# Rows of the input loads cut into two to six pieces, with a DRAM layout to match

## The chip, the cores and the metric

The kernel runs on one core of a Trainium2 chip. The metric is the device time of one execution, in microseconds (us). One profiled execution gives the trace; its clock starts at the first instruction.

## The reference

Three parts follow each other (float32 throughout): chunked attention with a few memory keys, a gated product without an activation, and a second feed-forward part with a SoLU and a layer norm.

```python
# attention: q, k, v (4, 8, 768, 64), mem_k, mem_v (4, 8, 8, 64); for each chunk of 32 queries:
scores = 0.125 * q_c @ concat(mem_k, k[chunk - 16 : chunk + 32 + 8]).T
a = exp(scores - max) ; a = a / (sum(a) + 1e-9) ; out_c = a @ concat(mem_v, v_ctx)
# x = out as (3072, 512)
x = ((x @ w_a) * (x @ w_b)) @ w_out            # d_ff 1536
h = x @ w_in                                    # 512 -> 1024
solu = h * softmax(h)
y = ((solu - mean) / sqrt(var + 1e-6) * g_ln) @ w_out2
```

## The kernel before

**Number format.** A float32 product is made of three passes with operands that are split into a high part and a rest (`w_hi` on ScalarE copies the high part, `w_lo` on VectorE subtracts it). The weights arrive as raw float64 words (512 of them are 4 KB) and are turned into float32 on the chip by integer steps: `abs` and `low` on ScalarE, `shl`, `sign` (or `join`) and `add` on VectorE, through a buffer `Z` with two halves that the weights use in turn, even and odd.

**Stages.** The first feed-forward part has 12 blocks f of 128 hidden columns. For each f there is one weight tile `raw` of 128 partitions by 1536 words (12 KB a partition, 1.5 MB): w_a, w_b and w_out side by side. The function `front` works on the first 512 tokens and converts all 12 weights on the way: products `pa`, `pb` with block f, the copy of the first product to `G` (step `G`), the gate (step `gate`), and the product `x` with w_out. Weights 0 and 1 come in three parts each (512 words a partition, 0.5 MB), weights 2 to 11 whole. The order of all this on TensorE, VectorE and ScalarE is written out by hand in the table `ORDER` (lines 45 to 66).

**Attention groups.** A group is 128 queries of all 8 heads: a query-key tile of 128 x 1280 float32 (5 KB a partition) and a value tile of 128 x 1024 (4 KB). Its steps are S (scores on TensorE), M (maximum and subtraction on VectorE), X (exponential on ScalarE), N (sums on VectorE, multiplication on VectorE or GpSimd), T (transposes on TensorE), A, V, C, L. Groups 0 to 3 run at the start, 4 to 7 inside `front`. After it pairs of groups are loaded by `pair_load`.

**Loads.** All loads and most stores are issued by SyncE in the order of the program; the data go through one queue over 16 DMA engines. Eight semaphores are used in turn, so a DMA is not issued before the eighth one ahead of it has landed. The first loads are, in order: qk0, qk1, weight 0 part 0, qk2, v0, weight 0 part 1, qk3, v1, weight 0 part 2, v2, weight 1 part 0, v3, weight 1 parts 1 and 2, weights 2, 3, 4, two stores of converted weights, weight 5, a store, weights 6 to 11, qk4, v4, qk5, then stores of converted weights (`w1_store`, lines 538 and 540), and the step `whole7` (line 517), which stores a third of `Z` to `woz`. The step `abs9` (line 421) writes that half of `Z` again, so it waits for that store.

Of the kernel before, what the change touches and what calls it, by code (L numbers as in the profile page):

```python
# [18 lines left out]
P = 128  # L19
B, H, S, D = 4, 8, 768, 64  # L20
# [3 lines left out]
NCH = 4  # L24
GQ = NCH * CQ
WQ = 2 * CQ
KW = 96
GK = GQ // WQ * KW
NG = S // GQ
NP = H // 2  # L30
DM = H * D
DFF1 = 1536
DFF2 = 1024
NF1 = DFF1 // P
# [4 lines left out]
WC = 512  # L39
# [33 lines left out]
NS = 3  # L73
# [7 lines left out]
def fused_kernel(  # L81
# [9 lines left out]
    nc = tc.nc  # L91
# [22 lines left out]
    def ld_tile(n, name):  # L114
        return ld_p.tile([P, n], F32, tag="ld", name=name, padded_shape=[P, NP * (GQ + GK)])
# [31 lines left out]
    def flat(t):  # L147
        return t.rearrange("p a c -> p (a c)")

    quads = {}  # L150
    rest = {}
    xt = {}
# [2 lines left out]
    def slot_tile(i, shape, dtype, name):  # L155

        return wp.tile(shape, dtype, tag=f"w{i}", name=name)
# [8 lines left out]
    def att_load(qi, slot=None):  # L166


        n = NP * (GQ + GK) + NCH * NP * D
        q, k = NP * GQ, NP * (GQ + GK)  # L170
        if slot is None:

            t = ld_tile(k, "qk")
            tv = ld_tile(n - k, "v")
        else:
            t = slot_tile(slot, [P, n], F32, "qkv")
            tv = t[:, k:n]
        nc.sync.dma_start(t[:, 0:k], qkv[qi, :, 0:k])
        quads[qi] = dict(
            q=t[:, 0:q].rearrange("d (p t) -> d p t", p=NP),  # L180
            k=t[:, q:k].rearrange("d (p t) -> d p t", p=NP),
            v=tv.rearrange("k (c p d) -> k c p d", c=NCH, p=NP),
        )

        def values():
            nc.sync.dma_start(tv, qkv[qi, :, k:n])

        if slot is None:
            values()
        return values  # L190

    def att_P(qi):
        full = ps_at.tile([P, 2, 512], F32, tag="at", name="s")
        s = full[:, :, 0:NP * CK].rearrange("q r (p k) -> q r p k", p=NP)
        if qi % NG == 0:
            nc.vector.memset(s[0:CQ, :, :, 0:16], NEG)
        if qi % NG == NG - 1:

            zero = ident[GQ - CQ:GQ, 0:8 * H].rearrange("q (r p k) -> q r p k", r=2, p=NP)
            nc.scalar.activation(  # L200
                out=s[GQ - CQ:GQ, :, :, 56:64], in_=zero, func=AF.Copy, scale=0.0, bias=NEG
            )
        quads[qi]["s"] = s

    def att_S(qi):


        st = quads[qi]
        g = qi % NG
        s = st["s"]  # L210
        for p in range(NP):
            for c in range(NCH):
                lo = 16 if (g == 0 and c == 0) else 0
                hi = 56 if (g == NG - 1 and c == NCH - 1) else CK
                k0 = (c // 2) * KW + (c % 2) * CQ
                for r in range(2):
                    rows = slice(64 * r, 64 * r + 64)
                    nc.tensor.matmul(  # L218
                        s[CQ * c:CQ * c + CQ, r, p, lo:hi],
                        st["q"][rows, p, CQ * c:CQ * c + CQ],  # L220
                        st["k"][rows, p, k0 + lo:k0 + hi],
                        start=True,
                        stop=True,
                    )
# [87 lines left out]
    def pair_load(d, i, values):  # L312

        qi = 2 * d + i
        n = NP * (GQ + GK) + NCH * NP * D
        q, k = NP * GQ, NP * (GQ + GK)
        if values:
            t = ld_tile(n - k, "v")
            nc.sync.dma_start(t, qkv[qi, :, k:n])
            quads[qi]["v"] = t.rearrange("k (c p d) -> k c p d", c=NCH, p=NP)  # L320
        else:
            t = ld_tile(k, "qk")
            nc.sync.dma_start(t, qkv[qi, :, 0:k])
            quads[qi] = dict(
                q=t[:, 0:q].rearrange("d (p t) -> d p t", p=NP),
                k=t[:, q:k].rearrange("d (p t) -> d p t", p=NP),
            )
# [149 lines left out]
    raws = {}  # L477
# [4 lines left out]
    def cols(part):  # L482
        return slice(0, NS * WC) if part is None else slice(part * WC, (part + 1) * WC)

    def w1_load(f, part=None):
        if f not in raws:
            raws[f] = slot_tile(f + 5 if f < PARTED else f, [P, NS * WC], I64, "raw")
        nc.sync.dma_start(raws[f][:, cols(part)], w1d[f, :, cols(part)])

    def w1_z(f, part=None):  # L490
        if f not in zs:
# [446 lines left out]
    def ab(bi, f, which, lo=0, hi=TB, ps=None, ks=range(NP)):  # L938
        xh, xl = xt[bi]
        w = wa1[f, which]  # L940
        if ps is None:
            ps = ps_ab.tile([P, TB], F32, tag=f"ps{which}", name="pab")
        sl = slice(lo, hi)
        for k in ks:
            mm3(ps[:, sl], w[:, 0, k], w[:, 1, k], xh[:, k, sl], xl[:, k, sl], k == 0, k == NP - 1)
        return ps
# [18 lines left out]
    def x2_step(bi, f, gh, gl, ms=range(NP)):  # L965
        if f == 0 and ms[0] == 0:
            acc[bi] = [ps_acc.tile([P, TB], F32, tag="acc", name="acc") for _ in range(NP)]
        w = wo1[f]
        for m in ms:
            sl = slice(m * P, (m + 1) * P)  # L970
            mm3(acc[bi][m], w[:, 0, sl], w[:, 1, sl], gh, gl, f == 0, f == NF1 - 1)
# [320 lines left out]
    values = {}  # L1292
# [21 lines left out]
    def front():  # L1314
        half = TB // 2
        psum = {}
        gates = {}
        started = {}
        q_end, k_end = NP * GQ, NP * (GQ + GK)

        def product(f, which, part):
            cols_, ks = started.get((f, which), (0, 0))
            if part == "l":
                started[f, which] = half, 0
                psum[f, which] = ab(0, f, which, 0, half)
                return
            to = NP // 2 if part == "h" else NP
            started[f, which] = cols_, to
            psum[f, which] = ab(0, f, which, cols_, ps=psum.get((f, which)), ks=range(ks, to))

        def add_x2(f, part):
            x2_step(0, f, *gates[f], ms=range(NP // 2) if part == "h" else range(NP // 2, NP))

        def group_S(q):
            if "s" not in quads[q]:
                att_P(q)
            att_S(q)

        def group_N(q):
            att_N(q, nc.vector if q < n0 else None)  # L1340

        def group_T(q):
            att_T(q, *((ps_ab, f"ps{q % 2}") if q < n0 else ()))

        def group_V(q):
            att_V(q, *((ps_acc, "acc") if q < n0 else ()))

        def load_qk(q):
            t = ld_tile(k_end, "qk")
            nc.sync.dma_start(t, qkv[q, :, 0:k_end])  # L1350
            quads[q] = dict(
                q=t[:, 0:q_end].rearrange("d (p t) -> d p t", p=NP),
                k=t[:, q_end:k_end].rearrange("d (p t) -> d p t", p=NP),
            )

        def load_v(q):
            n = NCH * NP * D
            t = ld_tile(n, "v")
            nc.sync.dma_start(t, qkv[q, :, k_end:k_end + n])
            quads[q]["v"] = t.rearrange("k (c p d) -> k c p d", c=NCH, p=NP)  # L1360

        def first(f):
            nc.scalar.copy(G0, psum[f, 0])  # L1363

        def second(f):
            gate_by(psum[f, 1])

        def gate_h(f):
            gates[f] = gate_hi(f)

        def gate_l(f):
            gate_lo(*gates[f])

        steps = dict(
            P=att_P, S=group_S, M=att_M, X=att_X, N=group_N, T=group_T, A=att_A, V=group_V, C=att_C, L=att_L,
            abs=w1_abs, neg=w1_neg, low=w1_low, shl=w1_shift, sign=w1_sign, join=w1_join,
            add=w1_add, hi=w1_hi, lo=w1_lo,
            G=first, gate=second, gh=gate_h, gl=gate_l,
            pa=lambda f, part=None: product(f, 0, part), pb=lambda f, part=None: product(f, 1, part),
            x=lambda f, part=None: add_x2(f, part),  # L1380
            loadw=w1_load, loadqk=load_qk, loadv=load_v,
            store=w1_store, whole=w1_whole,
            loadp=lambda i: pair_load(2 * NDIR, *((0, False), (1, False), (0, True))[i]),
        )
        def perform(item):
            name, *which = item.split(".")
            kind = name.rstrip("0123456789")
            steps[kind](int(name[len(kind):]), *(int(i) if i.isdigit() else i for i in which))

        for item in ORDER.split():  # L1390
            perform(item)
# [80 lines left out]
    for sb in range(NSB):  # L1472
        n = BASE[sb]
# [39 lines left out]
    for sb in range(NSB):  # L1513
# [24 lines left out]
        for p in range(HF):  # L1538
            a, b = order.index((2, p)), order.index((1, p))
# [82 lines left out]
    for sb in range(NSB):  # L1622
# [6 lines left out]
        for f in range(NF1):  # L1629
# [16 lines left out]
            v = bank_of("v", g)  # L1646
# [273 lines left out]
```

## Time and profile before

| | us |
|---|---|
| median of 3 runs (lowest to highest) | 874.55 (873.86 to 874.86) |
| the profiled execution's own time | 873.66 |
| its span, first to last instruction | 871.8 |
| TensorE busy | 855.4 (98%) |
| VectorE busy | 700.2 (80%) |
| ScalarE busy | 401.7 (46%) |
| GpSimd busy | 66.8 (8%) |

The shares are means over stages with different limits. The page has a row on the chain of work that ended last; the table by stretches shows what each engine does in each ten microseconds; the list of waits and the timeline show who waited for whom. Times of rows count from the span's start; 1.9 us of the execution lie outside the span.

### The profile page before, as it was taken

To read this page: it belongs to the slowest core of one execution; us is meant where nothing else is said; L and a number is where in the kernel's file an instruction comes from. 1 tells how busy PE (TensorE), PEld (TensorE's weight loads), DVE (VectorE), ACT (ScalarE), POOL (GpSimd) and SP (SyncE) were. 2 spreads that over 40 slices of the span, in tenths; PEclk is the share of its full clock that TensorE was granted. 3 is DMA by queue.
4 is the path that set the end of the run, shared out by engine and by line. 5 is a ranking of instruction groups with operands and counts; after the bars stand their busy time and mean duration, and the time that the engine had idled before them with its cause. 6 is when DMAs were issued, how large, how long until landed. Compare 5 with 4: busy or idle time off the path is not lost.

```text
span 871.8 us, 16681 instructions
## 1 busy us (share of the span) xinstructions
PE 855.4 (98%) x6696; PEld 707.3 (81%) x6696; DVE 700.2 (80%) x1136; ACT 401.7 (46%) x601; POOL 66.8 (8%) x79
## 2 busy tenths in 40 slices
PE   5999999999999999999999999999999999999998
PEld 4887878888888888888888888888888888888887
DVE  6999965978876685777957778999589999998892
ACT  5986432434343332334836544266354444444432
POOL 0001000000000000000000000000322223322110
PEclk9999999999999999999999999999999999999999
DMA  9997554967799679863889998468903555553343
GB/s 367 412 424 302 193 165 176 303 206 244 259 364 400 264 265 398 326 220 125 291 284 377 331 332 316 164 238 280 315 25 105 162 166 177 157 187 123 121 150 129
DMA packets 96542, 214.49 MB, mean 246 GB/s; under 512 B 7760, under 2 KB 58704, under 8 KB 91344
## 3 DMA queue, kind: packets, MB, share of 16 engines
q1 hardware_dynamic: 96432, 213.42, 68.9%
q8 instruction: 53, 0.87, 0.4%
q14 instruction: 25, 0.20, 0.1%
q0 software_dynamic: 32, 0.00, 0.0%
HBM read 147.85 MB, written 65.54 MB: 245 GB/s over the span
## 4 chain that ended last, share of the span: by engine, by line
PE 93%; DVE 4%; DMA 1%; ACT 1%; issue 1%; POOL 0%; ACTq 0%; DVEq 0%; POOLq 0%
PE acc L833 26%; PE pab L1275 15%; PE acc L1053 13%; PE pab L804 7%; PE acc L804 5%; PE pab L934 5%; PE pab L935 4%; PE pab L936 4%; PE acc L934 2%; PE acc L935 2%; PE acc L936 2%; PE px L399 2%; PE s L218 2%; PE px L287 1%; PE pab L833 1%; DMA w<-wos 1%
## 5 line engine op out<-in xcount | busy, mean ns | idle before, releaser
L833 PE MATMUL acc<-w 128*128 128x512 f32 x978 | 227.4, 390 | 0.0
L833 PEld LDWEIGHTS acc<-w 128*128 128x128 f32 x978 | 182.7, 188 | 38.1
L1275 PE MATMUL pab<-w 128*128 128x512 f32 (+1 forms) x600 | 134.3, 381 | 0.0
L1275 PEld LDWEIGHTS pab<-w 128*128 128x128 f32 x600 | 109.4, 188 | 21.9 <-DVE w L1252 0.3
L1001 POOL TENSOR_TENSOR w2ld<-w2ld 128x256 f32<-128x256 f32 x44 | 38.8, 902 | 528.5 <-ACT r L824 480.3
L934 PE MATMUL pab<-x,w 128*128 128x512 f32 (+1 forms) x200 | 78.7, 394 | 0.0
L935 PE MATMUL pab<-x,w 128*128 128x512 f32 (+1 forms) x200 | 76.9, 384 | 0.0
L936 PE MATMUL pab<-x,w 128*128 128x512 f32 (+1 forms) x200 | 76.8, 384 | 0.0
L804 PE MATMUL pab<-w 128*128 128x512 f32 x288 | 70.2, 390 | 0.2 <-DMA w<-wos 0.2
L846 DVE TENSOR_TENSOR part<-acc,part 128x512 f32<-128x512 f32 x56 | 38.6, 690 | 37.2 <-PE acc L833 28.4
L804 PEld LDWEIGHTS pab<-w 128*128 128x128 f32 x288 | 53.8, 188 | 11.7 <-ACT w L775 0.5
L1053 PE MATMUL acc<-w,hx 128*128 128x512 f32 x252 | 60.6, 390 | 0.1
L1053 PE MATMUL acc<-w 128*128 128x512 f32 x252 | 60.3, 390 | 0.0
L1053 PEld LDWEIGHTS acc<-w,hx 128*128 128x128 f32 x252 | 47.1, 188 | 10.2 <-DVE mx L1069 0.5
L1053 PEld LDWEIGHTS acc<-w 128*128 128x128 f32 x252 | 47.1, 188 | 9.7
L804 PE MATMUL acc<-w 128*128 128x512 f32 x216 | 51.7, 389 | 0.0
L804 PEld LDWEIGHTS acc<-w 128*128 128x128 f32 x216 | 40.5, 188 | 8.4
L934 PEld LDWEIGHTS pab<-x,w 128*128 128x128 f32 x200 | 38.1, 191 | 7.7 <-ACT G L1363 0.2
L936 PEld LDWEIGHTS pab<-x,w 128*128 128x128 f32 x200 | 38.1, 191 | 7.3
L935 PEld LDWEIGHTS pab<-x,w 128*128 128x128 f32 x200 | 38.2, 191 | 6.7
L779 DVE TENSOR_TENSOR w<-r,w 128x512 fp32r<-128x512 f32 x56 | 37.7, 688 | 1.9 <-ACT w L775 1.9
L934 PE MATMUL acc<-gh,w 128*128 128x512 f32 x96 | 38.2, 398 | 0.0
(234 smaller groups left out, 1392.4 us busy)
## 6 DMA issues: line engine op xcount, KB each, us to landing
w<-ws SPq DMA_DIRECT2D x24, 1024.0 KB, 7.3
w<-ws SPq DMA_DIRECT2D x24, 768.0 KB, 6.3
raw<-w1d_dram SPq DMA_DIRECT2D x10, 1536.0 KB, 16.4
qk<-qkv_dram SPq DMA_DIRECT2D x20, 640.0 KB, 6.1
ws<-Z SPq DMA_DIRECT2D x24, 512.0 KB, 4.5
w<-wos SPq DMA_DIRECT2D x48, 256.0 KB, 4.1
ztd<-r SPq DMA_DIRECT2D x84, 128.0 KB, 2.3
v<-qkv_dram SPq DMA_DIRECT2D x20, 512.0 KB, 5.4
```

The source lines that it names most:

```text
L218: nc.tensor.matmul(s[CQ * c:CQ * c + CQ, r, p, lo:hi], st["q"][rows, p, CQ * c:CQ * c + CQ], st["k"][rows, p, k0 + lo:k0 + hi], start=True ...
L399: nc.tensor.matmul(px[half:half + 64, r, p // 2, i, t], v[rows, c, p, :], at[rows, p, t], start=True, stop=True,)
L779: nc.vector.tensor_tensor(out=c[:, 1], in0=op_src(k), in1=c[:, 0].bitcast(F32), op=ALU.subtract)
L804: nc.tensor.matmul(ps, w[:, u, sl], g[:, v], start=first and n == 0, stop=last and n == 2, skip_group_check=True,)
L833: nc.tensor.matmul(ps, w[:, u, k], xx[v][:, k], start=(start and k == 0 and i == 0), stop=(stop and k == 1 and i == 2), skip_group_check=True,
L846: nc.vector.tensor_tensor(out=o, in0=a, in1=b, op=op)
L934: nc.tensor.matmul(ps, wl, xh, start=first, stop=False)
L935: nc.tensor.matmul(ps, wh, xl, start=False, stop=False)
L936: nc.tensor.matmul(ps, wh, xh, start=False, stop=last)
L1001: (nc.gpsimd if j else nc.vector).tensor_tensor(out=s4[:, i], in0=a, in1=b, op=op)
L1053: nc.tensor.matmul(ps, x, y, start=(start and k == 0 and i == 0), stop=(stop and k == 1 and i == 2), skip_group_check=True,)
L1275: nc.tensor.matmul(po, s[x][:, f], wo2(f)[:, h, sl], start=(m == 0), stop=(m == 3 * NF2 - 1))
```

## The change

The function that loads queries, keys and values, and the one that loads a first weight, read their DRAM tensor in pieces. On the host the arrays are laid out anew: all 128 first pieces of a load stand one behind the other, then all second pieces, and so on. The destination in SBUF is the same as before. A query-key tile comes in two pieces of 2.5 KB a partition, a value tile in two of 2 KB, a third of a weight in two of 2 KB, a whole weight in six of 2 KB. The loads of pairs (`pair_load`) change likewise.

```diff
     def flat(t):
         return t.rearrange("p a c -> p (a c)")
 
+    def load_qkv(t, qi, values=False):
+
+        n, at = (NCH * NP * D, P * NP * (GQ + GK)) if values else (NP * (GQ + GK), 0)
+        src = qkv[qi, at:at + P * n].rearrange("(a p n) -> p a n", a=2, p=P)
+        nc.sync.dma_start(t.rearrange("p (a n) -> p a n", a=2), src)
+
     quads = {}
     rest = {}
     xt = {}
...
         q, k = NP * GQ, NP * (GQ + GK)
         if values:
             t = ld_tile(n - k, "v")
-            nc.sync.dma_start(t, qkv[qi, :, k:n])
+            load_qkv(t, qi, True)
             quads[qi]["v"] = t.rearrange("k (c p d) -> k c p d", c=NCH, p=NP)
         else:
             t = ld_tile(k, "qk")
-            nc.sync.dma_start(t, qkv[qi, :, 0:k])
+            load_qkv(t, qi)
             quads[qi] = dict(
                 q=t[:, 0:q].rearrange("d (p t) -> d p t", p=NP),
                 k=t[:, q:k].rearrange("d (p t) -> d p t", p=NP),
...
     def w1_load(f, part=None):
         if f not in raws:
             raws[f] = slot_tile(f + 5 if f < PARTED else f, [P, NS * WC], I64, "raw")
-        nc.sync.dma_start(raws[f][:, cols(part)], w1d[f, :, cols(part)])
+        n = slice(0, 2 * NS) if part is None else slice(2 * part, 2 * part + 2)
+        nc.sync.dma_start(
+            raws[f][:, cols(part)].rearrange("p (a n) -> p a n", n=WC // 2),
+            w1d[f, n].rearrange("a p n -> p a n"),
+        )
 
     def w1_z(f, part=None):
         if f not in zs:
...
     )
     wab = np.stack([wa.reshape(NP, P, NF1, P), wb.reshape(NP, P, NF1, P)])
     wab = wab.transpose(3, 2, 0, 1, 4).reshape(NF1, P, 2 * DM)
+
+    def in_pieces(a, n):
+        return c(a.reshape(*a.shape[:2], n, -1).transpose(0, 2, 1, 3))
+
+    qk = np.concatenate([q.reshape(nq, P, NP * GQ), k.reshape(nq, P, NP * GK)], axis=2)
+    v = v.reshape(nq, P, NCH * NP * D)
     arrays = {
-        "qkv": np.concatenate(
-            [
-                q.reshape(nq, P, NP * GQ),
-                k.reshape(nq, P, NP * GK),
-                v.reshape(nq, P, NCH * NP * D),
-            ],
-            axis=2,
-        ),
-        "w1d": np.concatenate([wab, wo.reshape(NF1, P, DM)], axis=2),
+        "qkv": np.concatenate([in_pieces(qk, 2).reshape(nq, -1), in_pieces(v, 2).reshape(nq, -1)], axis=1),
+        "w1d": in_pieces(np.concatenate([wab, wo.reshape(NF1, P, DM)], axis=2), 2 * NS),
         "win2": wi2,
         "wout2": wo2,
         "gln": c(inputs["moe2_g_ln"].reshape(NF2, P).T),
```

No instruction changes place on any engine. On SyncE, at the start of the program, before (the shape is partitions x elements; `qkv`, `qk`, `v` are tiles of groups, `raw` is a weight, words of 8 bytes; `ws` is a store):

```order
L186 DMA qkv<-qkv_dram 128x1024
L488 DMA raw<-w1d_dram 128x512
L186 DMA qkv<-qkv_dram 128x1024
L488 DMA raw<-w1d_dram 128x512 x2
L488 DMA raw<-w1d_dram 128x1536 x3
L538 DMA ws_70<-w 128x1024
L540 DMA ws_70<-w 128x2x256
L488 DMA raw<-w1d_dram 128x1536
L538 DMA ws_71<-w 128x1024
L488 DMA raw<-w1d_dram 128x1536 x6
L1350 DMA qk<-qkv_dram 128x1280
L1359 DMA v<-qkv_dram 128x1024
```

The same place of SyncE after the change:

```order
L154 DMA qkv<-qkv_dram 128x2x512
L495 DMA raw<-w1d_dram 128x2x256
L154 DMA qkv<-qkv_dram 128x2x512
L495 DMA raw<-w1d_dram 128x2x256 x2
L495 DMA raw<-w1d_dram 128x6x256 x3
L548 DMA ws_70<-w 128x1024
L550 DMA ws_70<-w 128x2x256
L495 DMA raw<-w1d_dram 128x6x256
L548 DMA ws_71<-w 128x1024
L495 DMA raw<-w1d_dram 128x6x256 x6
L154 DMA qk<-qkv_dram 128x2x640
L154 DMA v<-qkv_dram 128x2x512
```

Nothing moved; only the shapes of the loads differ, and with them the number of rows that each one is made of.

## Rows read from the trace of the kernel before

**Rows 1.** The page: shares of the chain that ended last.
```profile
PE 93%; DVE 4%; DMA 1%; ACT 1%; issue 1%; POOL 0%; ACTq 0%; DVEq 0%; POOLq 0%
```
**Rows 2.** Busy time by stretches of 10 us; the first row names the columns.
```profile
core 0: us, PE busy (x) PEld busy (x) DVE busy (x) ACT busy (x) POOL busy (x), PEclk, DMA share, GB/s
...
50.00:60.00 10.00, 10.00 (x46) 8.29 (x45) 10.00 (x10) 8.52 (x8) 0.00 (x0) 1.00 1.00 428
...
80.00:90.00 10.00, 9.66 (x105) 7.69 (x104) 9.38 (x11) 5.96 (x7) 2.37 (x1) 1.00 0.38 131
...
580.00:590.00 10.00, 9.85 (x44) 7.85 (x43) 9.36 (x16) 8.75 (x17) 0.00 (x0) 1.00 1.04 375
```
**Rows 3.** Timeline at 80 us: start, us, engine, line, operation, [idle before].
```profile
80.33 1.61 ACT L421 ACTIVATE Z<-raw 128x1536 f32<-128x1536 f32 x1 [3.15 <-DMA woz<-Z]
...
81.83 0.58 ACT L1363 COPY G<-pab 128x512 f32<-128x512 f32 x1
82.49 0.60 ACT L239 ACTIVATE EB<-s 128x512 f32<-128x512 f32 x1
...
82.63 0.69 DVE L949 TENSOR_TENSOR G<-G,pab 128x512 f32<-128x512 f32 x1 [0.23 <-PE pab L936]
...
86.94 0.66 PE L260 MATMUL pt<-ident,EB 128*128 128x128 f32 x4 [0.34 <-POOL EB L250]
```
**Rows 4.** The chain that ended last, 60 to 130 us: start, us, what.
```profile
110.85 0.43 PE pab L934
```
**Rows 5.** The store of `whole7`, line 517: issue, and time to landing.
```profile
L517 SPq DMA_DIRECT2D woz<-Z x1: 320/320/320, 75.2 to 75.2; - x1
...
DMA to landing us min/median/max: 5.1/5.1/5.1
```
**Rows 6.** The page: packets; queues (packets, MB, share); issues (KB each, us to landing).
```profile
DMA packets 96542, 214.49 MB, mean 246 GB/s; under 512 B 7760, under 2 KB 58704, under 8 KB 91344
...
q1 hardware_dynamic: 96432, 213.42, 68.9%
q8 instruction: 53, 0.87, 0.4%
q14 instruction: 25, 0.20, 0.1%
...
w<-ws SPq DMA_DIRECT2D x24, 1024.0 KB, 7.3
...
raw<-w1d_dram SPq DMA_DIRECT2D x10, 1536.0 KB, 16.4
...
wos<-r SPq DMA_DIRECT2D x6, 1024.0 KB, 6.6
```
**Rows 7.** Weight loads, line 488: four from 4.7 us, six from 34.5.
```profile
L488 SPq DMA_DIRECT2D raw<-w1d_dram x4: 328/328/443, 4.7 to 11.9; - x4
...
DMA to landing us min/median/max: 11.9/12.1/12.8
...
L488 SPq DMA_DIRECT2D raw<-w1d_dram x6: 332/434/466, 34.5 to 37.0; - x6
...
DMA to landing us min/median/max: 12.0/20.1/28.0
```
**Rows 8.** Timeline of ScalarE: two first reads of weights (columns as rows 3).
```profile
17.87 0.69 ACT L432 ACTIVATE raw<-raw 128x512 int32<-128x512 uint32 x1
...
52.41 1.65 ACT L432 ACTIVATE raw<-raw 128x1536 int32<-128x1536 uint32 x1
```
**Rows 9.** SyncE: loads of 512 pieces (ns min/median/max); the issue after the weights.
```profile
L986 SPq DMA_DIRECT2D w2ld<-x2d x12: 529/533/1435, 583.2 to 779.2; - x12
...
41.61 0.33 SPq L1350 DMA_DIRECT2D qk<-qkv_dram  x1
```
**Rows 10.** The chain in the first 30 us: shares by line; first piece.
```profile
by line: DMA qkv<-qkv_dram 12.8%; DVE EB L250 9.3%; PE px L287 9.3%; DVE sm L247 9.0%; issue 8.1%; PE pt L260 7.3%; DVE mx L229 6.4%; ACT EB L239 6.1%; DVE s L230 4.9%; DVE Z L463 4.6%; PE s L218 3.9%; DVE sm L249 2.9%; PE pab L935 2.9%; PE
...
0.74 3.85 DMA qkv<-qkv_dram
```

More of the change, by code (lines that the diff above doesn't have):

```diff
@@ L177, in att_load @@
             tv = t[:, k:n]
-        nc.sync.dma_start(t[:, 0:k], qkv[qi, :, 0:k])
+        load_qkv(t[:, 0:k], qi)
         quads[qi] = dict(
@@ L185, in values @@
         def values():
-            nc.sync.dma_start(tv, qkv[qi, :, k:n])
+            load_qkv(tv, qi, True)
         if slot is None:
@@ L1349, in load_qk @@
             t = ld_tile(k_end, "qk")
-            nc.sync.dma_start(t, qkv[q, :, 0:k_end])
+            load_qkv(t, q)
             quads[q] = dict(
@@ L1358, in load_v @@
             t = ld_tile(n, "v")
-            nc.sync.dma_start(t, qkv[q, :, k_end:k_end + n])
+            load_qkv(t, q, True)
             quads[q]["v"] = t.rearrange("k (c p d) -> k c p d", c=NCH, p=NP)
```

## The prediction

> **What bounds the kernel now.** I read the page first. The chain that ended last is TensorE for 93% of the span [rows 1], so the change can matter only where TensorE, or what it waits for, waits in its turn for a load. The table by stretches [rows 2] shows where loads could do that: at 50 to 60 us the 16 DMA engines are full (share 1.00, 428 GB/s) while TensorE is busy all the time, and at 80 to 90 they no longer are (0.38), while TensorE loses 0.34 us. So a full queue of loads runs through the first 80 us with the compute behind it, and the question is what hangs on the end of this queue.
>
> The timeline answers it: at 80.33 us ScalarE has stood idle 3.15 us for a DMA, the store of `Z` to `woz` [rows 3]. The waiting instruction is `abs9` (it overwrites the half of `Z` that `whole7` is still storing), and behind it in ScalarE's order stand the copy of `G` at 81.83 and the exponential of group 4 at 82.49. The chain says what they lead to: the gate on VectorE at 82.63, the sums of group 4, GpSimd's normalisation, TensorE's transposes at 86.94 (for which it sat idle the 0.34 us), and on in short steps over several engines until TensorE has it again at 110.85 [rows 3, 4]. Slack in front of it: the copy of `G` ends at 81.83 + 0.58 = 82.41, the gate starts at 82.63, so `abs9` could come about 0.2 us later for nothing. Everything beyond that is passed on. The store itself was issued at 75.2 and landed 5.1 us later, at 80.3 [rows 5]: it stood at the end of the full queue.
>
> **What the change does, and its cost.** No instruction changes place, and no byte is added. Each load of queries, keys and values becomes two pieces per partition (2.5 or 2 KB), each third of a first weight two (2 KB), each whole first weight six (2 KB, before one of 12 KB). In the trace a row is one DMA packet: 10 x 128 rows of 12 KB, 24 x 128 of 8 KB (`w<-ws`) and 6 x 128 of 8 KB (`wos<-r`) are 5120, and with the 53 and 25 instruction packets that makes 5198, just what 96542 minus the 91344 under 8 KB leaves [rows 6]. So the change adds packets, and the price is what a packet costs beside its bytes.
>
> That price can be read off two runs of loads in the full queue. The load issued at 4.7 landed 12.8 us later (17.5), the one at 11.9 landed 11.9 later (23.8); in the program's order five loads of 512 KB end in between (values, weight third, values, two weight thirds): 6.3 / 5 = 1.26 us each, with rows of 4 KB [rows 7]. Of the six whole weights, the one issued at 34.5 landed after 12.0 (46.5), the one at 37.0 after 28.0 (65.0): 18.5 / 5 = 3.70 us each, rows of 12 KB [rows 7]. Each of 16 engines carries 8 rows: 157.5 ns for a 4 KB row, 462.5 ns for a 12 KB row. The difference is 38.1 ns per KB, so 4 KB of bytes are 152.5 ns, and 5.0 ns is left per packet. Reading a landing to 0.05 us makes this 5 +- 2.5 ns.
>
> The Trainium skill (DMA: Bandwidth & Descriptors, "Why small descriptors are slow") speaks against the change in the same sense: a fixed overhead of some 3 cycles for every packet. By that and its fabric clock of 850 MHz my estimate would be 3.5 ns, 1.9 us in the sum below in place of 2.7, which after the 0.2 us of slack is 1.7; the rows give 5.0, and I go by the rows.
>
> Ahead of the `woz` store in the queue, per engine: six query-key and five value loads, 11 x 8 = 88 more packets; six weight thirds, 6 x 8 = 48; ten whole weights, 10 x 40 = 400; together 536. 536 x 5.0 ns = 2.7 us. The store lands at 83.0 in place of 80.3, 0.2 us of that is slack, 2.5 us go on to the chain.
>
> The bounds of that cost. Below: nothing, if 5.0 ns is a reading error. Above: the nearest long stretch full of short rows is 580 to 590 us (rows of 1, 2 and 4 KB, reads mixed with stores), 375 GB/s at a share of 1.04 [rows 2]. That is 23.4 GB/s per engine, 87.4 ns for 2 KB, 76.2 of them bytes: 11.2 ns per packet, 6.0 us. I take 5.0, because its rows are loads from the same tensors in the same queue, while the other stretch holds 1 KB rows and stores.
>
> What I cost at nothing:
> - The loads that ScalarE reads earlier. The tightest are the third read at 17.87 (landed 17.5; 72 more packets by then, 0.36 us) and the whole weight read at 52.41 (landed 46.5 + 3.7 = 50.2; 352 packets, 1.8 us of 2.2) [rows 7, 8]. Both just fit; at 11.2 ns they would be 0.4 and 1.7 us late, but the later wait for `woz` is set by the queue and swallows a delay before it.
> - SyncE's issue. A load of 128 rows takes 0.328 us to issue at least, one of 512 pieces 0.533 [rows 7, 9], so some 0.53 ns a piece, and 768 pieces about 0.67 us. Six weights in a row cost 2.0 us more, so that the last, issued at 37.0, would be through by some 39.5; the next issue is at 41.6 [rows 9], when weight 5 has landed and its semaphore is free. Without that cover a query-key load would be issued late that nobody reads before 80 us.
> - The first load. It is on the path (3.85 us) [rows 10]; 128 more pieces make its issue 0.07 us longer, and half a row less to wait for is at most 0.1 us the other way.
> - The 32 loads of the pairs from 120 to 370 us: no wait there is for them, and 8 packets are 0.04 us.
>
> Sum against the profiled execution: 873.66 + 2.5 = 876.2 us. The median of the runs shown is 0.9 us above that execution, so the forecast is 874.55 + 2.5 = 877.0 us. A measurement of this kernel can tell about 0.2% from no change, 1.75 us here; 2.5 us is 0.28%.
>
> **Rivals.**
> - *No cost for a piece of 2 KB.* If an engine fetches the next piece while it still writes the last, the 5.0 ns vanish, or fall under 3.6 ns (1.95 us, where the 1.75 us begins). For it: a share above 1.00 (1.04 at 580 us) says that packets overlap already. Against it: the 375 GB/s of short rows. The same result comes if the pieces are put together again on the way. Time 874.5; up to 876.3 it counts as no change.
> - *Short pieces are much dearer.* 11 ns or near it: 6.0 - 0.2 = 5.8 us, 880.4. For it the stretch at 580, against it the 4 KB loads at 1.26 us.
> - *Faster: instruction blocks get through.* TensorE's program comes in packets of 0.87 MB / 53 = 16.4 KB through the same 16 engines [rows 6], and in the first 30 us the chain holds 8.1% of "issue", 2.4 us [rows 10]. If a block waits behind whole rows, shorter rows shorten the wait; if all of it went, 2.4 us: 872.1. It decides only from 1.75 us on, and only if the queue does not slow at all, for `abs9` waits for the queue's end whatever the front gains. The Trainium skill (Runtime: NRT & Kernel Launch, "Instruction fetch mechanics") gives blocks of 16 KiB, as the row shows, and calls their cost mostly hidden; the gaps here are not proof of either. Against it: in the first 25 us rows are only 4 to 5 KB, 0.2 us each.
>
> **How the numbers follow.** Forecast (packet cost 3.6 to about 8 ns): 0.43. Much dearer: 0.12. No cost, or under 3.6 ns: 0.36. Faster: 0.09. So slower 0.55, same 0.36, faster 0.09. The range of 8 in 10 leaves out the whole faster rival and most of the upper tail: 873.6 (no cost, and a little gained in the front) to 880.0. If the cost is there, the forecast's own range is 876.3 to 878.7.
>
> **What the profile would show.** The DMA queue's packets rise from 96432 by 13312 (48 loads x 128, 6 x 128, 10 x 640) to about 109,700, and those of 8 KB and more fall by 1280; if not, the change does not do what it says. Six whole weights land 3.9 us apart instead of 3.70, the last at about 67.6 instead of 65.0. `abs9` starts near 83.0, ScalarE's wait there is near 5.9 us, and TensorE's idle time before the transposes at 86.94 becomes some 2.8 us at 89.4. From 111 us on, every instruction is later by the same 2.5 us. The prediction is wrong if the weights land 3.70 us apart or less, if the first 30 us lose their "issue" gaps, or if `abs9` is late and the transposes are not.

## The result, and the profile after

The changed kernel takes 878.78 us (median of 4 runs, 878.53 to 880.89) against 874.2 us before (4 runs, 873.81 to 874.86): ratio 1.0058, 95% interval 1.0046 to 1.0070. That is 4.6 us slower, where 2.5 were forecast; the time lies in the stated range of 873.6 to 880.0, just above the 876.3 to 878.7 that the forecast gave for itself. The profiled execution took 878.92 us, its span is 877.2 us, 5.4 more than before.

On the page, the chain that ended last has less of TensorE than before (87% instead of 93%) and more of DMA, and the packets are counted [rows 1, 6]:

```profile
PE 87%; DVE 6%; ACT 3%; DMA 3%; issue 2%; POOL 0%; ACTq 0%; DVEq 0%; POOLq 0%; SPq 0%
...
DMA packets 109854, 214.49 MB, mean 245 GB/s; under 512 B 7760, under 2 KB 58704, under 8 KB 105936
...
q1 hardware_dynamic: 109744, 213.42, 69.7%
```

The queue has 109744 - 96432 = 13312 packets more, exactly the number of pieces added, and the same bytes. Packets of 8 KB and more went from 5198 to 3918, the 1280 whole-weight rows.

The timeline at the end of the queue (columns as in rows 3):

```profile
84.43 1.58 ACT L427 ACTIVATE Z<-raw 128x1536 f32<-128x1536 f32 x1 [7.42 <-DMA woz<-Z]
85.90 0.59 ACT L1373 COPY G<-pab 128x512 f32<-128x512 f32 x1
86.37 0.62 ACT L245 ACTIVATE EB<-s 128x512 f32<-128x512 f32 x1
...
86.53 0.69 DVE L959 TENSOR_TENSOR G<-G,pab 128x512 f32<-128x512 f32 x1 [4.33 <-ACT G L1373]
86.55 0.50 PE L944 MATMUL pab<-x,w 128*128 128x512 f32 x1 [1.47 <-ACT G L1373]
...
90.83 1.12 PE L266 MATMUL pt<-ident,EB 128*128 128x128 f32 x4 [2.63 <-POOL EB L256]
```

`abs9` starts at 84.43 instead of 80.33, after a wait of 7.42 us instead of 3.15. Everything behind it moved as one block: the copy of `G` by 4.07 us, the gate by 3.9, the transposes by 3.9. TensorE waited 1.47 us for the copy of `G`, which it did not before, and 2.63 for the transposes instead of 0.34.

The load of the first whole weight of the six and that of the last, and the store that `abs9` waits for [rows 5, 7]:

```profile
L495 SPq DMA_DIRECT2D raw<-w1d_dram x1: 1708/1708/1708, 35.1 to 35.1; - x1
...
DMA to landing us min/median/max: 13.4/13.4/13.4
...
L495 SPq DMA_DIRECT2D raw<-w1d_dram x1: 3890/3890/3890, 52.0 to 52.0; - x1
...
DMA to landing us min/median/max: 16.8/16.8/16.8
...
L527 SPq DMA_DIRECT2D woz<-Z x1: 332/332/332, 77.3 to 77.3; - x1
...
DMA to landing us min/median/max: 7.0/7.0/7.0
```

35.1 + 13.4 = 48.5 and 52.0 + 16.8 = 68.8: six weights land 20.3 / 5 = 4.06 us apart, before 3.70. The store lands at 84.3, before 80.3. The six loads are now issued over 17 us, where they were issued within 2.5 us.

Of the 4.0 us, 2.1 lie ahead of the store's issue (77.3, before 75.2) and 1.9 behind it (7.0 us to landing, before 5.1). SyncE's waits for this store at 60 to 80 us (us in total, times, longest), before and after, tell why:

```profile
SPq L517 <- DVE Z L463: 2.0, 1, 2.0
...
SPq L527 <- DMA ws<-w: 0.8, 1, 0.8
```

Before, SyncE last waited for VectorE, which was still making the `Z` to be stored. In the changed kernel it waited for the store eight places ahead to land, so that the issue, too, follows the queue.

By stretches, the engines are full for longer at a lower rate, and the last rows show something that was not forecast (columns as in rows 2):

```profile
50.00:60.00 10.00, 10.00 (x46) 8.29 (x45) 10.00 (x10) 8.63 (x8) 0.00 (x0) 1.00 1.05 387
80.00:85.00 5.00, 5.00 (x82) 3.87 (x77) 1.96 (x3) 0.57 (x1) 0.00 (x0) 1.00 1.04 396
85.00:90.00 5.00, 1.73 (x7) 1.05 (x6) 3.41 (x6) 2.71 (x5) 1.59 (x1) 1.00 0.18 68
90.00:95.00 5.00, 4.17 (x14) 3.51 (x15) 4.93 (x4) 2.54 (x3) 0.78 (x1) 0.66 0.14 52
...
91.00:94.00 3.00, 3.00 (x10) 2.52 (x11) 2.95 (x3) 0.97 (x2) 0.00 (x0) 0.50 0.14 54
```

387 GB/s stand against 428 in the same ten microseconds. At 85 to 90 us TensorE is busy 1.73 of 5 us, and right after that its granted clock is 0.66 on average, and 0.50 (the level of 1.2 GHz) from 91 to 94. ScalarE's exponential of group 5, before and after:

```profile
102.96 0.60 ACT L239 ACTIVATE EB<-s 128x512 f32<-128x512 f32 x1
...
108.01 0.59 ACT L245 ACTIVATE EB<-s 128x512 f32<-128x512 f32 x1
```

The delay has grown from the 3.9 us of the gate and the transposes to 5.05 us, and from there to 430 us it stays at 5.1.

### The profile page after: what moved, and what is told of

Its sections match the earlier page's. It is cut to its first block, busy times and chain, and to the rows that moved or that the text cites. A ratio compares the mean times of both kernels' runs of the same rounds, so it can differ in the third digit from the quotient of the medians.

```text
span 877.2 us, 16681 instructions
## 1 busy us (share of the span) xinstructions
PE 857.4 (98%) x6696; PEld 708.2 (81%) x6696; DVE 700.7 (80%) x1136; ACT 402.2 (46%) x601; POOL 67.0 (8%) x79
## 3 DMA queue, kind: packets, MB, share of 16 engines
q1 hardware_dynamic: 109744, 213.42, 69.7%
## 4 chain that ended last, share of the span: by engine, by line
PE 87%; DVE 6%; ACT 3%; DMA 3%; issue 2%; POOL 0%; ACTq 0%; DVEq 0%; POOLq 0%; SPq 0%
PE acc L843 25%; PE pab L1285 15%; PE acc L1063 13%; PE pab L814 7%; PE acc L814 5%; PE pab L944 4%; PE pab L946 3%; PE pab L945 3%; PE acc L944 2%; PE px L405 2%; PE acc L946 2%; PE acc L945 2%; PE s L224 2%; DMA ws<-w 1%; DVE Z L469 1%
```

## The experiments

**Theory A:** a packet costs some 7.5 ns beside its bytes (4.03 us / 536), the full queue ends later by that, `abs9` waits for its end, and TensorE's clock adds about 1 us after the long wait. **Rivals:** the new order in DRAM makes the reads slow; what counts are the first loads of the program; SyncE, held up in its issues, is late for something.

**The pieces without the new order.** Pieces of the same size, but a partition's pieces stand one behind the other, with gaps that keep them apart:

```diff
-            w1d[f, n].rearrange("a p n -> p a n"),
+            w1d[f, :, n, 0:WC // 2],
...
-        return c(a.reshape(*a.shape[:2], n, -1).transpose(0, 2, 1, 3))
+        a = a.reshape(*a.shape[:2], n, -1)
+        return np.pad(a, ((0, 0), (0, 0), (0, 0), (0, 512 // a.itemsize)))
```

> Pieces as in the change (2 to 2.5 KB), but each partition's pieces lie one behind the other in DRAM as before, with 512 bytes between them so that they stay separate. Theory (a packet costs some 7.5 ns beside its bytes, 536 more of them per engine stand ahead of the woz store): the store lands near 84.3 us as in the changed kernel, time 4 to 5.5 us above before. Rival (the new order in DRAM slows the reads): the store lands near 80.3 as before, whole weights 3.70 us apart, time within 1 us of before.

Measured: 878.66 us, ratio 1.0046 (1.0031 to 1.0061). The store is issued at 77.3 and lands 7.1 us later, at 84.4:

```profile
L528 SPq DMA_DIRECT2D woz<-Z x1: 332/332/332, 77.3 to 77.3; - x1
...
DMA to landing us min/median/max: 7.1/7.1/7.1
```

The order in DRAM makes no difference that shows; the pieces do. This execution had no fall of the clock, and TensorE reached its faster pace only at 35.0 us (below). It is a control for the clock: TensorE's transposes behind the same wait are 3.9 us late here as well, but group 5's exponential is still only 3.9 us late, where it was 5.05 with the clock at 0.50.

```profile
106.87 0.59 ACT L246 ACTIVATE EB<-s 128x512 f32<-128x512 f32 x1
```

The execution still ends 5.0 us later than before's profiled one; the other 1.1 us come after 250 us, and no run explains them.

**Only the whole weights cut.** The six pieces for weights 2 to 11 alone:

```diff
+PIECES_Q, PIECES_THIRD, PIECES_WHOLE = 1, 1, 6
...
+        k = PIECES_THIRD * NS if f < PARTED else PIECES_WHOLE
...
+            w1d[f].rearrange("(a p n) -> p a n", a=k, p=P)[:, n],
```

> Only the ten whole weights come in six pieces; queries, keys, values and the thirds of weights 0 and 1 in one, as before. Theory: 400 of the 536 packets, 400 x 7.5 ns = 3.0 us, the store lands near 83.3, 2.8 us of it on the path, and up to 1.7 us more if TensorE's clock falls after the wait: 2.8 to 4.5 us above before. Rival (it is the first loads of the program that count): under 1 us above before.

Measured: 876.88 us, ratio 1.0033 (1.0021 to 1.0045), 2.9 us above before. The store lands at 75.7 + 7.0 = 82.7, half a microsecond earlier than forecast. TensorE lost 0.39 us at 80 to 85 us and 2.63 at 85 to 90, and then the clock fell as well:

```profile
80.00:85.00 5.00, 4.61 (x40) 3.40 (x21) 1.48 (x4) 2.16 (x3) 0.00 (x0) 1.00 0.88 340
85.00:90.00 5.00, 2.37 (x12) 1.72 (x13) 4.93 (x7) 2.57 (x4) 2.37 (x1) 1.00 0.15 57
90.00:95.00 5.00, 5.00 (x71) 3.81 (x70) 4.93 (x4) 1.09 (x2) 0.00 (x0) 0.66 0.00 0
```

**Only the rest cut.** Queries, keys, values and thirds in two pieces, whole weights in one:

```diff
+PIECES_Q, PIECES_THIRD, PIECES_WHOLE = 2, 2, 1
```

> The rest of the change: queries, keys, values and thirds in two pieces, whole weights in one row of 12 KB. Theory: 136 packets, 1.0 us, the store lands near 81.3, time 0.8 us above before, no fall of the clock. Rival (the first loads count): 3 us or more above before.

Measured: 875.03 us, ratio 1.0007 (0.9997 to 1.0016), 1.0 us above before and not clear of noise. The store lands at 76.4 + 4.5 = 80.9, 0.6 us later than before, and the clock does not fall. The two halves of the change, 2.9 and 1.0 us, make most of its 4.6, the second of them not clear of noise. The rival of the first loads falls.

This run's profiled execution was the longest of its ten (876.02 us), and its trace says why: at 33 us TensorE's matmuls of 256 columns take 0.41 us, where before (first two lines) they take 0.28.

```profile
33.11 0.28 PE L935 MATMUL pab<-x,w 128*128 128x256 f32 x1
33.23 0.28 PE L936 MATMUL pab<-x,w 128*128 128x256 f32 x1
...
33.27 0.41 PE L947 MATMUL pab<-x,w 128*128 128x256 f32 x1
33.48 0.41 PE L948 MATMUL pab<-x,w 128*128 128x256 f32 x1
...
104.86 0.59 ACT L246 ACTIVATE EB<-s 128x512 f32<-128x512 f32 x1
```

They start 0.21 us apart, before 0.12. The first of them at the faster pace stands at 34.7 us here, at 35.0 with the gaps, and at 30.6 and 30.5 us in the traces of before and after, though the granted clock reads 1.00 in all of them. TensorE is 1.9 us behind the trace of before by 46 us and still 1.9 at group 5's exponential (last line, against 102.96). So in this trace the store's 0.6 us cost nothing on top, and how much of the run's 1.0 us the pieces made is not shown.

**The store ahead.** The changed kernel, with four stores of converted weights behind `whole7` in the order table:

```diff
-    pb4.h gl3 sign6 G4 pb4 low9 lo5 x3.h add6 store5.0 store5.1 x3 abs7 pa5.h gate4 hi6 shl7 pa5
-    gh4 lo6 low10 pb5.h gl4 store6.0 store6.1 abs8 pb5 sign7 x4.h G5 add7 low11 x4 gate5 whole7
...
+    pb4 low9 lo5 x3.h add6 x3 abs7 pa5.h gate4 hi6 shl7 pa5 gh4 lo6 low10 pb5.h gl4 abs8 pb5 sign7
+    x4.h G5 add7 low11 x4 gate5 whole7 store5.0 store5.1 store6.0 store6.1 hi7 shl8 pa6.h gh5 lo7
```

> The changed kernel, and in the table ORDER the four stores of converted weights 5 and 6 stand behind the step whole7 instead of ahead of it, so 1.5 MB less stands in the queue before the woz store. Theory (the time is lost where abs9 waits for that store): the store lands near 80.5 although the loads are as slow as in the changed kernel, ScalarE waits about 3 us instead of 7.4, time within 0.6 us of before. Rivals (late weights, or SyncE held up by its long issues, cost the time): 3 us or more stay.

Measured: 873.89 us, ratio 0.9995 (0.9984 to 1.0005). The loads are as slow as in the changed kernel (387 GB/s at 50 to 60 us, issues of the last six weights of 1.1 to 6.0 us), but the store is issued at 74.8 and lands after 5.1 us, and the wait is as long as before:

```profile
79.92 1.61 ACT L426 ACTIVATE Z<-raw 128x1536 f32<-128x1536 f32 x1 [3.14 <-DMA woz<-Z]
81.43 0.57 ACT L1372 COPY G<-pab 128x512 f32<-128x512 f32 x1
82.06 0.60 ACT L244 ACTIVATE EB<-s 128x512 f32<-128x512 f32 x1
```

All of the 4.6 us are back. So they were lost at this one wait, and neither the late weights nor SyncE's long issues cost anything that shows beside it. That the move by itself gains nothing, the next run shows.

**The same move in the kernel before.** The same words of the table moved:

> The kernel before, with the four stores of weights 5 and 6 behind the step whole7. Theory: ScalarE's wait of 3.15 us for the woz store goes, but the exponential behind it then waits for VectorE's subtraction that ends at 82.40, so at most 0.2 us is gained: no change that can be measured. Rival (the wait was worth its length): 2 to 3 us below before.

Measured: 873.85 us, ratio 0.9999 (0.9988 to 1.0010). The wait for the store is gone, and the time is not:

```profile
78.06 1.63 ACT L420 ACTIVATE Z<-raw 128x1536 f32<-128x1536 f32 x1 [1.31 <-DVE w L469]
79.58 0.58 ACT L1362 COPY G<-pab 128x512 f32<-128x512 f32 x1
82.03 0.60 ACT L238 ACTIVATE EB<-s 128x512 f32<-128x512 f32 x1 [1.86 <-DVE s L229]
```

The exponential now waits 1.86 us for VectorE. In the kernel before, 3.15 us of waiting stood on the edge of costing something, and cost nothing.

**Three pieces, and twelve.** Whole weights alone, in three pieces of 4 KB (`PIECES_WHOLE = 3`), and in twelve of 1 KB (`PIECES_WHOLE = 12`).

> Only the ten whole weights are cut, in three pieces of 4 KB. Theory (each packet costs some 8 ns whatever its size): 16 more packets per load and engine, whole weights 3.70 + 0.13 = 3.83 us apart, 160 packets ahead of the woz store, 1.3 us, the store lands near 81.5, time about 1.0 us above before. Rival (only pieces under about 4 KB cost, since 4 KB rows ran as fast per byte as 12 KB rows): 3.70 to 3.75 us apart, time within 0.4 us of before.

> Only the ten whole weights are cut, in twelve pieces of 1 KB: the suspected cost doubled. Theory: 88 more packets per load and engine, 3.70 + 0.70 = 4.40 us apart; 880 packets ahead of the woz store, 7 us, the store lands near 87.3, time 6.8 to 8.5 us above before. Rival (the making of pieces by the issuing side is the limit, and doubles from 6 to 12 pieces): a DMA share well under 1 in the first 80 us and more than 5 us between weights.

Measured: three pieces 874.66 us, ratio 1.0007 (0.9998 to 1.0016); twelve 881.76 us, ratio 1.0090 (1.0077 to 1.0104), 7.9 us above before. The store lands at 81.2 and 86.6. With twelve pieces the engines are not short of work; their share is above 1 and their rate lower:

```profile
50.00:60.00 10.00, 10.00 (x45) 8.28 (x45) 10.00 (x10) 8.11 (x8) 0.00 (x0) 1.00 1.10 348
...
85.00:90.00 5.00, 1.19 (x6) 0.97 (x6) 1.16 (x2) 3.00 (x4) 0.00 (x0) 1.00 0.75 291
90.00:95.00 5.00, 2.65 (x10) 1.75 (x9) 4.90 (x7) 2.25 (x3) 2.37 (x1) 0.51 0.14 52
```

So the making of pieces is not the limit. The first and the last of the last six weights, with three pieces and with twelve:

```profile
L497 SPq DMA_DIRECT2D raw<-w1d_dram x1: 372/372/372, 34.0 to 34.0; - x1
...
DMA to landing us min/median/max: 12.7/12.7/12.7
...
L497 SPq DMA_DIRECT2D raw<-w1d_dram x1: 3487/3487/3487, 45.2 to 45.2; - x1
...
DMA to landing us min/median/max: 20.8/20.8/20.8
...
L497 SPq DMA_DIRECT2D raw<-w1d_dram x1: 985/985/985, 37.0 to 37.0; - x1
...
DMA to landing us min/median/max: 11.9/11.9/11.9
...
L497 SPq DMA_DIRECT2D raw<-w1d_dram x1: 4379/4379/4379, 56.7 to 56.7; - x1
...
DMA to landing us min/median/max: 14.7/14.7/14.7
```

The spacing, from the landing of the first and of the last of them (45.2 + 20.8 is rounded twice; by the nanoseconds of the trace this weight lands at 65.90):

| pieces of a whole weight | first and last of six land at, us | apart, us | per added packet, ns |
|---|---|---|---|
| 1 (12 KB, before) | 46.5, 65.0 | 3.70 | |
| 3 (4 KB) | 46.7, 65.9 | 3.84 | 8.8 |
| 6 (2 KB, after) | 48.5, 68.8 | 4.06 | 9.0 |
| 12 (1 KB) | 48.9, 71.4 | 4.50 | 9.1 |

The last column is the added time over the packets added per engine (16, 40, 88). The price is the same from 4 KB down to 1 KB; the rival that only short pieces cost falls too. By the nanoseconds of the traces the four spacings are 3.691, 3.839, 4.064 and 4.499 us, 9.2 to 9.3 ns for each added packet. They repeat: 3.687 and 3.686 in the two other traces with whole rows, 4.065 to 4.066 in the three others with six pieces. The Trainium skill (DMA: Bandwidth & Descriptors, "Why small descriptors are slow") has the sign right with its 3 cycles a packet. At the 850 MHz that the Trainium skill gives there (section "Specifications") that is an estimate of 3.5 ns a packet; these runs show 9.

## Why the prediction was right, and where it was off

**The place: right.** The front follows the end of the full queue at one point, the wait of `abs9` for the `woz` store. With the loads slow and that store ahead the loss is gone, and with the loads fast and that store ahead nothing is gained. The store itself was taken to be issued at 75.2 as before; it was issued 2.1 us later, held by the queue.

**The packets: right.** 13312 more, one for each piece.

**The price of a packet: the step that failed in size.** The prediction took 5.0 ns from 4 KB rows in 1.26 us loads and 12 KB rows in 3.70 us loads; the runs show 9 ns in the loads of whole weights. What is left per packet is 1.5 times the time of a 4 KB row minus half the time of a 12 KB row, so the 157.5 ns read for 4 KB, where the three-piece run shows 3.84 us / 24 = 160, made 5.0 out of 8.8. Most of it is rounding. In the nanoseconds of the same trace the two landings are at 17.46 and 23.82 us, in place of 17.5 and 23.8, and the six weights land 3.691 us apart: 159.0 and 461.4 ns a row, and 7.8 ns is left per packet. The error of 2.5 ns that the prediction gave is that of one row of 4 KB; it left out the factor of 1.5.

**The sum of the queue: 4.0 us in place of 2.7.** 536 packets at 9 ns would be 4.8 us; the store was 4.0 us late, 7.5 ns a packet. The 0.8 us between are not settled. By the landings in the traces the changed kernel is 2.2 us late at weight 4, 1.6 at weight 5 and 3.8 at weight 11, so 0.7 us were given back between weights 4 and 5, where two stores of converted weights stand in the queue. And at 76 to 80 us, while the `woz` store was waiting, the engines were no longer full before (first line), but still were in the changed kernel:

```profile
76.00:80.00 4.00, 4.00 (x19) 3.10 (x17) 3.92 (x4) 1.18 (x2) 0.00 (x0) 1.00 0.72 274
...
76.00:80.00 4.00, 4.00 (x34) 3.06 (x39) 3.91 (x4) 1.02 (x2) 0.00 (x0) 1.00 1.05 408
```

One profile of each kernel does not tell how much each of these made; the third of weight 0 lands anywhere from 17.0 to 18.3 us in these traces.

**The slack of 0.2 us, and that the rest is passed on: right.** The copy of `G` moved by 4.07 us, the gate and the transposes by 3.9.

**What was missing: TensorE's clock.** The prediction let every later instruction be late by the same amount, and put no term for the clock in its sum. The amount grew by 1.15 us behind the transposes at 90.83, where the granted clock was 0.50 after TensorE had lost 1.47 and 2.63 us; in the run with gaps, where the clock stayed at 1.00 behind the same wait, it did not grow. With 4.1 us at `abs9`, 0.2 of slack taken off and 1.15 of clock the profiled execution is at 5.05 of its 5.3 us. The rest comes after 430 us and is not explained, and before's own runs spread over 2 us and more.

**The number.** 878.8 is 1.8 us above the forecast of 877.0 and 1.6 below the 880.4 of the dearer piece. The direction and the path came as forecast; the size was short by 1.3 us of queue and 1.15 of clock. That the time still lies in the stated range owes something to the room that was left there for the dearer piece.

**The loads that ScalarE reads earlier: nearly right.** The prediction had weight 7 land 1.8 us later and just fit. It landed 2.3 us later, and ScalarE waited 0.2 us for it, which the wait for `woz` swallowed.

**SyncE's issue: wrong, at no cost.** 0.67 us was forecast for a load of 768 pieces; the first of them took 0.48, the last six, in the full queue, 1.7 to 6.0 us. The engines stayed full meanwhile (share 1.02 to 1.06 from 8 to 84 us), so what SyncE held up would have stood in the same queue anyway, and the run with the store ahead shows that nothing else was lost.

**The rivals.** That a piece costs nothing is out, and so is that the change does not do what it says. Faster by shorter gaps of "issue" is out: in the first 30 us they are 8.3% of the chain, before 8.1%. The dearer piece, put at 11 ns, was the nearest in price; its 5.8 us were more than the 4.6 that the runs gave, and 1.15 of these were the clock's.

## What to carry to other kernels

A load that is hidden behind compute still has a price per row where the DMA queue is full: multiply the packets by what one costs (here 7.5 to 9 ns per engine) and look at what waits at the end of that queue, which may be a store that has nothing to do with the loads. A wait of several microseconds can be worth nothing (taking it away gained nothing here) and yet stand on the edge, so that each further microsecond counts in full. Where a short store is waited for, look at its place in the order of issues first: here the move of four stores behind it gave back all that the slower loads had cost. And a small difference of large times, such as the price of a packet, wants landings read to the nanosecond.

## What the runs showed of the hardware that was not expected

- Each added packet cost about 9 ns of each engine's time in the full queue, the same for rows of 4, 2 and 1 KB (8.8, 9.0, 9.1 ns).
- An issue of SyncE held its engine while the queue was full of small pieces: 1.7 to 6.0 us for each of the last six loads of 768 pieces, before 0.33 to 0.47 us for one of 128 rows.
- TensorE's granted clock fell to 0.50 after waits of 4.1 us in sum (after) and of 3.0 us (whole weights only), and was 0.51 from 90 to 95 us with twelve pieces; it stayed at 1.00 after waits of 2.1 us (pieces with gaps).
- At the start TensorE came to its faster pace by 30.6 us in some traces and only at 34.7 or 35.0 us in two others, with the granted clock at 1.00 in all; in one of the two TensorE was then 1.9 us behind, and stayed so.
